# Attention products per head in 32-column tiles, V in chunks of 128 tokens, packs in two loads

## The chip, the cores and the metric

One core of one Trainium2 chip runs the whole program. The metric is the device time of one execution in microseconds (us). On the core, TensorE (PE in the profile; PEld is its loading of the stationary operand), VectorE (DVE), ScalarE (ACT), GpSimd (POOL) and SyncE (SP, which issues most DMAs) each work through a list of instructions in order and wait for each other by semaphores.

## What is computed

Three layers follow each other: attention through packs, a mixture of 4 experts with given weights, and a mixture of 8 experts of which each token takes two. The change is in the first.

```python
def _attn_ref(q, k, v, p):          # q, k, v: (4, 8, 576, 64); p: (4, 8, 32, 64)
    def sm_attn(qq, kk, vv):
        s = scale * np.matmul(qq, kk.transpose(0, 1, 3, 2))
        a = np.exp(s - np.max(s, axis=-1, keepdims=True))
        a = a / (np.sum(a, axis=-1, keepdims=True) + 1e-09)
        return np.matmul(a, vv)
    p_packed = sm_attn(p, k, v)
    return sm_attn(q, p_packed, p_packed)
```

For each of 4 batches and 8 heads, 32 packs attend to 576 tokens, and then the 576 tokens attend to the 32 packs. The result, 2304 tokens by 512, goes through both mixtures, whose products are made in two-part float32 (`mm3`, three fp32r matmuls for each product). The attention's own products are plain float32.

## The kernel before

The attention is cut into eight units (`Attn`, one batch `b` and one group `g` of four heads). a0 to a3 are the units of batches 0 and 1; `at_u` holds the four units of batches 2 and 3. A group is two pairs of heads: `hl` is the pair, `h2` the head in it. Since 128 partitions hold two heads of 64 numbers, one matmul over 128 rows works on a pair, and the 128 output rows hold four heads by 32 packs.

A unit has stages. `load_p` (L209) loads the packs (`pc`, 32 KB) and GpSimd spreads them into a zeroed tile `self.p` (L214, L219), so that a pair's matmul writes zeros to the rows of the other pair and the two pairs add up in one PSUM tile. `s1` (L233) makes the scores of the packs, two halves of 288 tokens with two matmuls each, then maximum (DVE) and exponential (ACT). `ext` (L254) transposes the exponentials on TensorE, in five chunks of CH = 116 tokens (the last has 112), and ACT copies them to `a1t`. `pv` (L266) multiplies by v, five matmuls of 256 columns: each head's row meets all four heads' v, and L272 scales and multiplies by a mask that keeps each head's own 64 columns. `pt` (L275) transposes the result, two transposes, and ACT and GpSimd make the tiles `PTr`, `PTh`, `PTl` of it; `PTr` has a zeroed middle part, so that `s2a` (L289) can take 128 columns of it with zeros on one side and add the two pairs up. `s2a` gives the scores of the tokens; `s2b` to `s2f` are the softmax over 32 packs with 32x32 transposes on DVE and the two-part split into `AT`, which the first mixture reads.

Two places hold all this. In the start, ahead of the first mixture, the code calls the stages of a0 to a3 and the first weights' loads (`w_load`, L123, SP) and splits (`w_split`: ACT makes the high part at L68, GpSimd or VectorE the low part at L69) in an order written by hand (L389 to L451). Then the main loop of the first mixture runs, and a list of places (`at(place, f)`) puts the rest between its steps: s2a to s2f of a2 and a3, and all stages of the four units in `at_u` (L481 to L494), so four times s1, ext, pv and pt and six times s2a stand in the stream of the mixture's matmuls (L63 to L65). Every load goes through SP's one queue in the order of the calls.

Of the kernel before, what the change touches and what calls it, by code (L numbers as in the profile page):

```python
# [22 lines left out]
CH, NC = 116, 5  # L23
# [5 lines left out]
def tile_pack_attn_moe_moe(ctx: ExitStack, tc: tile.TileContext, qT, kT, pT, vv, dp, noise,  # L29
# [13 lines left out]
    def acc_ps(t=0):  # L43
        # the fifth bank is free for other work while four tiles are summed
        if t == 4:
            return ps.tile([128, 512], F32, name="accx", tag="accx", bufs=1)
        return ps.tile([128, 512], F32, name="acc", tag="acc", bufs=4)
# [24 lines left out]
    ident = consts.tile([128, 128], F32, name="ident")  # L72
    mask = [consts.tile([128, 256], F32, name=f"mask{i}") for i in range(2)]
# [10 lines left out]
    def early_consts():  # L84
        make_identity(nc, ident)
        for par in range(2):
            nc.gpsimd.memset(mask[par], 0.0)
            for slot in range(2):
                for h2 in range(2):
                    c = ((slot ^ par) * 2 + h2) * 64  # L90
                    r = slot * 64 + h2 * 32
                    nc.gpsimd.memset(mask[par][r:r + 32, c:c + 64], 1.0)
# [40 lines left out]
    # step i: 0..127 first mixture, 200..239 its last tiles, 300.. second mixture  # L133
# [53 lines left out]
    # =====================================================================  # L187
# [4 lines left out]
    def pt_alloc(bp):  # L192
        for hp in range(4):
            r = atp.tile([128, 3, 64], F32, name="ptr", tag=f"ptr{hp}", bufs=1)
            nc.gpsimd.memset(r[:, 1, :], 0.0)
            PTr[bp, hp] = r
# [3 lines left out]
    class Attn:  # L200
        """One batch, four heads: rows (slot, head of the pair, pack) of the two pairs."""
# [7 lines left out]
        def load_p(self):  # L209
            b, g = self.b, self.g  # L210
            pc = self.t([2, 32], "pc")
            nc.sync.dma_start(pc, pT[b, :, 2 * g:2 * g + 2, :])
            self.p = self.t([2, 128], "pT")
            nc.gpsimd.memset(self.p, 0.0)  # L214
            for hl in range(2):
                for h2 in range(2):
                    c = (hl ^ (b % 2)) * 64 + h2 * 32
                    r = slice(h2 * 64, h2 * 64 + 64)
                    nc.gpsimd.tensor_copy(self.p[r, hl, c:c + 32], pc[r, hl, :])  # L219
# [13 lines left out]
        def s1(self):  # L233
            o = [self.new_ps() for _ in range(2)]
            for i in range(2):
                for hl in range(2):
                    nc.tensor.matmul(o[i][:, :288], self.p[:, hl, :], self.k[:, hl, i * 288:(i + 1) * 288],
                                     start=hl == 0, stop=hl == 1)
# [15 lines left out]
        def ext(self):  # L254
            a = self.t([NC, 128], "a1t", CH)
            self.a1t = a
            o = self.new_ps()
# [8 lines left out]
        def pv(self):  # L266
            o = self.new_ps()
            for c in range(NC):
                r = CH if c < 4 else S - 4 * CH
                nc.tensor.matmul(o[:, :256], self.a1t[:r, c, :], self.v[:r, c, :], start=c == 0, stop=c == NC - 1)  # L270
            self.pm = self.t([256], "pm")
            nc.vector.scalar_tensor_tensor(self.pm, o[:, :256], self.sm[:, 7:8], mask[self.b % 2],  # L272
                                           op0=OP.mult, op1=OP.mult)

        def pt(self):  # L275
            o = self.new_ps()
            bp = self.b // 2
            for hl in range(2):
                nc.tensor.transpose(o[:, hl * 128:(hl + 1) * 128], self.pm[:, hl * 128:(hl + 1) * 128], ident)
            for hl in range(2):  # L280
                s = hl ^ (self.b % 2)
                hp = 2 * self.g + hl
                src = o[:, hl * 128 + s * 64:hl * 128 + s * 64 + 64]
                nc.scalar.activation(PTr[bp, hp][:, 2 * s, :], src, AF.Copy)
# [782 lines left out]
```

## Time and profile before

| | |
|---|---|
| three runs | 1268.83, 1271.12, 1272.71 us; median 1271.12 |
| span of the profiled execution | 1268.5 us (its own time is not listed) |
| TensorE busy | 1220.7 us, 96% |
| DVE, ACT, POOL busy | 38%, 37%, 39% |
| DMA | 121.24 MB, mean 96 GB/s |
| chain that ended last | PE 82%, DMA 8%, DVE 4% |

How to read it: the span is the time from the first to the last instruction of one execution. The busy share is a mean over the whole program, and a matmul's busy time includes its way through the array, so that matmuls in a stream overlap in the record: the distance of their starts, not their duration, is what one costs there. The chain goes back from the last instruction to what released it, step by step.

### The profile page before, as it was taken

The page shows a single profiled execution, that of the slowest core. Times are in us where ns is not written, and L with a number is a line of the kernel's source. Part 1 is how long each engine was busy: PE and PEld are TensorE (multiplying, and loading weights), DVE is VectorE, ACT ScalarE, POOL GpSimd, SP SyncE. Part 2 cuts the span into 40 slices and gives each one's busy share as a digit, 9 for nine tenths or more (in the row PEclk, how much of TensorE's full clock was granted, in tenths as well). Part 3 has the DMA queues.
Part 4 walks back from the last instruction along what each step waited for, and adds up shares of the span by engine and source line. Part 5 has one row for each costly group of instructions (what it writes and reads, how often), then busy time and mean ns, then how long its engine had stood idle before and what let it go on. Part 6 is the DMA issues. An engine that isn't in the chain of part 4 may idle for free.

```text
span 1268.5 us, 17265 instructions
## 1 busy us (share of the span) xinstructions
PE 1220.7 (96%) x6638; PEld 1060.8 (84%) x6638; DVE 482.3 (38%) x1183; ACT 467.6 (37%) x973; POOL 489.5 (39%) x377
## 2 busy tenths in 40 slices
PE   4789999999999999999999998799999999999997
PEld 2578888888888898888888887689998998989986
DVE  1564333433464622454435345452212132222222
ACT  1453543433433543634425333342233333232321
POOL 2323322312332411314613134234575757557554
PEclk7999999999999999999999999899999999999999
DMA  5331321321221311212242204454252544535332
GB/s 151 107 128 34 89 86 37 105 81 41 96 80 34 125 51 34 67 34 67 37 67 67 66 20 115 129 168 149 74 173 81 168 135 137 170 116 177 114 140 76
DMA packets 51624, 121.24 MB, mean 96 GB/s; under 512 B 18683, under 2 KB 18827, under 8 KB 51537
## 3 DMA queue, kind: packets, MB, share of 16 engines
q1 hardware_dynamic: 41536, 99.97, 26.0%
q0 software_dynamic: 10000, 20.11, 4.9%
q8 instruction: 55, 0.90, 0.3%
q14 instruction: 33, 0.26, 0.1%
HBM read 105.64 MB, written 23.31 MB: 102 GB/s over the span
## 4 chain that ended last, share of the span: by engine, by line
PE 82%; DMA 8%; DVE 4%; issue 2%; ACT 2%; POOL 1%; SPq 0%; DVEq 0%; POOLq 0%; ACTq 0%
PE acc L64 12%; PE acc L63 12%; PE acc L65 12%; PE mm L63 11%; PE mm L65 11%; PE mm L64 11%; PE accx L64 2%; PE accx L65 2%; PE accx L63 2%; DMA qk<-in_kT_dram 2%; DMA gt<-yd,mti 2%; DMA meta<-rr,rsi 1%; PE mm L828 1%; DMA raw<-in_w_dram 1%; DMA raw<-in_m_dram 1%
## 5 line engine op out<-in xcount | busy, mean ns | idle before, releaser
L69 POOL TENSOR_TENSOR w1l<-raw,w1h 128x1024 fp32r<-128x1024 f32 x58 | 139.5, 2405 | 336.2 <-ACT w1h L68 317.2
L69 POOL TENSOR_TENSOR w2l<-raw,w2h 128x1024 fp32r<-128x1024 f32 x61 | 146.5, 2401 | 217.5 <-ACT w2h L68 179.3
L63 PE MATMUL acc<-w2h,hh 128*128 128x512 f32 x448 | 182.0, 406 | 0.9 <-DVE ml L368 0.9
L64 PE MATMUL acc<-w2l,hh 128*128 128x512 f32 x448 | 177.9, 397 | 0.5 <-DVE w2l L69 0.5
L65 PE MATMUL acc<-w2h,hl 128*128 128x512 f32 x448 | 176.9, 395 | 0.0
L500 DVE SCALAR_TENSOR_TENSOR gl<-mm,gh 128x320 fp32r<-128x320 f32 (+2 forms) x128 | 62.9, 491 | 264.2 <-ACT gh L499 264.1
L499 ACT ACTIVATE gh<-mm 128x320 fp32r<-128x320 f32 (+2 forms) x128 | 56.0, 437 | 282.8 <-PE mm L65 282.8
L63 PE MATMUL mm<-xth,w1h 128*128 128x320 f32 (+2 forms) x512 | 158.7, 310 | 0.9 <-DVE gl L500 0.9
L64 PE MATMUL mm<-xtl,w1h 128*128 128x320 f32 (+2 forms) x512 | 158.1, 309 | 0.6 <-DVE xtl L69 0.6
L65 PE MATMUL mm<-xth,w1l 128*128 128x320 f32 (+2 forms) x512 | 157.9, 308 | 0.0
L63 PE MATMUL mm<-ath,mh 128*128 128x288 f32 x512 | 152.5, 298 | 1.0 <-ACT mh L366 0.7
L65 PE MATMUL mm<-ath,ml 128*128 128x288 f32 x512 | 151.2, 295 | 2.1 <-DVE ml L368 2.1
L64 PE MATMUL mm<-atl,mh 128*128 128x288 f32 x512 | 151.2, 295 | 0.0
L500 DVE SCALAR_TENSOR_TENSOR hl<-mm,hh 128x224 fp32r<-128x224 f32 (+1 forms) x256 | 102.0, 421 | 93.3 <-ACT hh L499 92.8
L368 DVE TENSOR_TENSOR ml<-mm,mh 64x512 fp32r<-64x512 f32 x120 | 82.6, 689 | 120.1 <-ACT mh L366 119.6
L499 ACT ACTIVATE hh<-mm 128x224 fp32r<-128x224 f32 (+1 forms) x256 | 91.2, 384 | 93.4 <-PE mm L65 71.0
L63 PE MATMUL acc<-w2h,gh 128*128 128x512 f32 x264 | 108.0, 409 | 3.6 <-ACT gh L499 3.6
L65 PE MATMUL acc<-w2h,gl 128*128 128x512 f32 x264 | 105.1, 398 | 2.0 <-DVE gl L500 2.0
L64 PE MATMUL acc<-w2l,gh 128*128 128x512 f32 x264 | 104.8, 397 | 0.0
L63 PEld LDWEIGHTS mm<-ath,mh 128*128 128x128 f32 x512 | 96.1, 188 | 8.1 <-ACT mh L366 1.1
L65 PEld LDWEIGHTS acc<-w2h,hl 128*128 128x128 f32 x448 | 84.2, 188 | 20.4
L64 PEld LDWEIGHTS mm<-atl,mh 128*128 128x128 f32 x512 | 96.2, 188 | 5.4
(237 smaller groups left out, 2173.7 us busy)
## 6 DMA issues: line engine op xcount, KB each, us to landing
raw<-in_m_dram SPq DMA_DIRECT2D x72, 512.0 KB, 3.6
raw<-in_w_dram SPq DMA_DIRECT2D x64, 512.0 KB, 4.0
yd<-y SPq DMA_DIRECT2D x7, 1280.0 KB, 8.1
v<-in_vv_dram SPq DMA_DIRECT2D x8, 580.0 KB
qk<-in_kT_dram SPq DMA_DIRECT2D x8, 576.0 KB, 4.6
qk<-in_qT_dram SPq DMA_DIRECT2D x8, 576.0 KB, 3.6
x2d<-x SPq DMA_DIRECT2D x18, 256.0 KB, 5.1
xg<-x2d,mti POOLq DMA_INDIRECT x40, 4.0
```

Source lines behind the costliest of these rows:

```text
L63: nc.tensor.matmul(o, ah, bh, start=start, stop=False)
L64: nc.tensor.matmul(o, ah, bl, start=False, stop=False)
L65: nc.tensor.matmul(o, al, bh, start=False, stop=stop)
L69: (eng or nc.vector).tensor_sub(l, x, h.bitcast(F32))
L368: nc.vector.tensor_sub(l[r, g, :], o[r, :], h[r, g, :].bitcast(F32))
L499: nc.scalar.activation(hd, src, AF.Relu)
L500: nc.vector.scalar_tensor_tensor(ld, src, 0.0, hd.bitcast(F32), op0=OP.max, op1=OP.subtract)
L828: nc.tensor.transpose(o[:, d * 128:(d + 1) * 128], XG[j][t][:, d * 128:(d + 1) * 128], ident)
```

## The change

Each head's products are made by themselves. A matmul of s1, pv and s2a now takes 32 columns of stationary operand (one head's packs) and writes 32 of the 128 output rows (`heads()` gives the pair, the head and the rows). The packs come from the host with zeros where the other head of the pair stands, for all units in one tile `pall`, in two loads of 256 KB: batches 0 and 1 ahead of all loads, batches 2 and 3 at the end of the start. GpSimd's spreading of the packs and the zeroed middle of `PTr` are gone. v is cut into chunks of 128 tokens (the last has 64, padded with zeros by the host; GpSimd zeroes the rows of `a1t` that go with them). The mask now only puts a head's 64 columns into the left or right half, and `pt` needs one transpose.

```diff
-CH, NC = 116, 5
+CH, NC = 128, 5
-    mask = [consts.tile([128, 256], F32, name=f"mask{i}") for i in range(2)]
+    mask = consts.tile([128, 2, 64], F32, name="mask")
+    pall = consts.tile([128, NB, 4, 2, 32], F32, name="pall")
...
-            r = atp.tile([128, 3, 64], F32, name="ptr", tag=f"ptr{hp}", bufs=1)
-            nc.gpsimd.memset(r[:, 1, :], 0.0)
-            PTr[bp, hp] = r
+            PTr[bp, hp] = atp.tile([128, 2, 64], F32, name="ptr", tag=f"ptr{hp}", bufs=1)
...
-        def load_p(self):
-            b, g = self.b, self.g
-            pc = self.t([2, 32], "pc")
-            nc.sync.dma_start(pc, pT[b, :, 2 * g:2 * g + 2, :])
-            self.p = self.t([2, 128], "pT")
-            nc.gpsimd.memset(self.p, 0.0)
+        def heads(self):
             for hl in range(2):
                 for h2 in range(2):
-                    c = (hl ^ (b % 2)) * 64 + h2 * 32
-                    r = slice(h2 * 64, h2 * 64 + 64)
-                    nc.gpsimd.tensor_copy(self.p[r, hl, c:c + 32], pc[r, hl, :])
+                    q = 2 * (hl ^ (self.b % 2)) + h2
+                    yield hl, h2, slice(q * 32, q * 32 + 32)
...
             for i in range(2):
-                for hl in range(2):
-                    nc.tensor.matmul(o[i][:, :288], self.p[:, hl, :], self.k[:, hl, i * 288:(i + 1) * 288],
-                                     start=hl == 0, stop=hl == 1)
+                for hl, h2, r in self.heads():
+                    nc.tensor.matmul(o[i][r, :288], pall[:, self.b, 2 * self.g + hl, h2, :],
+                                     self.k[:, hl, i * 288:(i + 1) * 288], start=True, stop=True)
...
             a = self.t([NC, 128], "a1t", CH)
             self.a1t = a
+            nc.gpsimd.memset(a[S - 4 * CH:, 4, :], 0.0)
...
             for c in range(NC):
-                r = CH if c < 4 else S - 4 * CH
-                nc.tensor.matmul(o[:, :256], self.a1t[:r, c, :], self.v[:r, c, :], start=c == 0, stop=c == NC - 1)
-            self.pm = self.t([256], "pm")
-            nc.vector.scalar_tensor_tensor(self.pm, o[:, :256], self.sm[:, 7:8], mask[self.b % 2],
-                                           op0=OP.mult, op1=OP.mult)
+                for hl, h2, r in self.heads():
+                    h = (2 * hl + h2) * 64
+                    nc.tensor.matmul(o[r, :64], self.a1t[:, c, r], self.v[:, c, h:h + 64],
+                                     start=c == 0, stop=c == NC - 1)
+            self.pm = self.t([2, 64], "pm")
+            nc.vector.scalar_tensor_tensor(self.pm, o[:, :64].unsqueeze(1).to_broadcast([128, 2, 64]),
+                                           self.sm[:, 7:8], mask, op0=OP.mult, op1=OP.mult)
...
-            for hl in range(2):
-                nc.tensor.transpose(o[:, hl * 128:(hl + 1) * 128], self.pm[:, hl * 128:(hl + 1) * 128], ident)
+            nc.tensor.transpose(o[:, :128], self.pm.rearrange("p a j -> p (a j)"), ident)
...
             for i in range(2):
-                for hl in range(2):
-                    s = hl ^ (b % 2)
-                    r = PTr[bp, 2 * g + hl].rearrange("p a j -> p (a j)")
-                    nc.tensor.matmul(self.o2[i][:, :288], r[:, s * 64:s * 64 + 128],
-                                     self.q[:, hl, i * 288:(i + 1) * 288], start=hl == 0, stop=hl == 1)
+                for hl, h2, r in self.heads():
+                    nc.tensor.matmul(self.o2[i][r, :288], PTr[bp, 2 * g + hl][:, hl ^ (b % 2), h2 * 32:h2 * 32 + 32],
+                                     self.q[:, hl, i * 288:(i + 1) * 288], start=True, stop=True)
...
+        nc.sync.dma_start(pall[:, 0:2], pT[:, 0:2])
         for u in (a0, a1):
-            u.load_p()
             u.load_k()
             u.load_v()
...
         w_load(("w1", 0, 3), w1_src(0, 3))
+        nc.sync.dma_start(pall[:, 2:], pT[:, 2:])
```

SP's queue at the start of the program before; pc is a unit's packs, qk its k or q, v its v, raw a weight:

```order
1 L212 DMA pc<-in_pT_dram 128x64
2 L223 DMA qk<-in_kT_dram 128x1152
3 L227 DMA v<-in_vv_dram 116x1280
4 L212 DMA pc<-in_pT_dram 128x64
5 L223 DMA qk<-in_kT_dram 128x1152
6 L227 DMA v<-in_vv_dram 116x1280
7 L212 DMA pc<-in_pT_dram 128x64 [waits DMAHW0_49,Pool_49]
8 L223 DMA qk<-in_kT_dram 128x1152
9 L231 DMA qk<-in_qT_dram 128x1152
10 L212 DMA pc<-in_pT_dram 128x64 [waits DMAHW3_49,DMAHW1_49,Pool_49]
11 L223 DMA qk<-in_kT_dram 128x1152 [waits DMAHW2_49,PE_49]
12 L123 DMA raw<-in_w_dram 128x1024
```

And with the change:

```order
1 L387 DMA pall<-in_pT_dram 128x512
2 L213 DMA qk<-in_kT_dram 128x1152
3 L217 DMA v<-in_vv_dram 128x1280
4 L213 DMA qk<-in_kT_dram 128x1152
5 L217 DMA v<-in_vv_dram 128x1280
6 L213 DMA qk<-in_kT_dram 128x1152
7 L221 DMA qk<-in_qT_dram 128x1152
8 L213 DMA qk<-in_kT_dram 128x1152 [waits DMAHW1_49,PE_49]
9 L120 DMA raw<-in_w_dram 128x1024 [waits DMAHW0_49]
10 L217 DMA v<-in_vv_dram 128x1280 [waits DMAHW2_49,PE_49]
11 L221 DMA qk<-in_qT_dram 128x1152 [waits DMAHW3_49]
12 L120 DMA raw<-in_w_dram 128x1024
```

The four small loads became one ahead of everything, v has 128 rows in place of 116, and the loads of a2 no longer wait for GpSimd.

TensorE's list in the main loop, around the first s1 there (accx, acc and mm are PSUM tiles, w2h and w2l a weight's two parts); before:

```order
531 L64 MATMUL acc<-w2l,hh 128x512
532 L65 MATMUL acc<-w2h,hl 128x512
533 L237 MATMUL accx<-qk,pT 128x288 x2
534 L237 MATMUL mm<-qk,pT 128x288 x2
535 L63 MATMUL acc<-w2h,hh 128x512
```

And with the change:

```order
531 L64 MATMUL acc<-w2l,hh 128x512
532 L65 MATMUL acc<-w2h,hl 128x512
533 L227 MATMUL accx<-qk,pall 32x288 x4
534 L227 MATMUL mm<-qk,pall 32x288 x4
535 L63 MATMUL acc<-w2h,hh 128x512
```

The place is the same; four products of 128 output rows became eight of 32 rows with the same 288 columns each.

## Rows read from the trace of the kernel before

**Rows 1.** The page's busy times, and TensorE's busy share in 40 slices.

```profile
PE 1220.7 (96%) x6638; PEld 1060.8 (84%) x6638; DVE 482.3 (38%) x1183; ACT 467.6 (37%) x973; POOL 489.5 (39%) x377
...
PE   4789999999999999999999998799999999999997
```

**Rows 2.** Table by stretches: us, busy (instructions) per engine, clock, DMA share, GB/s.

```profile
0.00:63.50 63.50, 39.63 (x143) 26.71 (x143) 21.63 (x60) 18.80 (x56) 19.38 (x55) 0.84 0.47 129
100.00:420.00 320.00, 319.90 (x1677) 274.78 (x1676) 137.40 (x314) 130.65 (x311) 84.55 (x69) 1.00 0.22 69
```

**Rows 3.** The chain of waits in the start: start us, us, what.

```profile
3.93 23.37 DMA qk<-in_kT_dram
...
34.71 12.52 DMA raw<-in_w_dram
...
47.25 1.07 ACT w1h L68
```

**Rows 4.** Table by stretches, in the start.

```profile
2.00:12.00 10.00, 5.15 (x16) 2.34 (x14) 1.70 (x7) 1.11 (x5) 1.13 (x5) 0.97 0.93 226
14.00:18.00 4.00, 0.47 (x1) 0.50 (x2) 0.00 (x0) 0.00 (x0) 1.50 (x7) 0.50 0.25 90
24.00:30.00 6.00, 2.56 (x6) 1.88 (x7) 0.51 (x3) 0.35 (x2) 1.96 (x9) 0.59 0.26 101
...
76.00:80.00 4.00, 3.30 (x19) 2.50 (x17) 2.61 (x3) 2.31 (x4) 0.00 (x0) 1.00 0.99 391
```

**Rows 5.** DMA issues: count, size of each, us to landing.

```profile
raw<-in_w_dram SPq DMA_DIRECT2D x64, 512.0 KB, 4.0
...
v<-in_vv_dram SPq DMA_DIRECT2D x8, 580.0 KB
qk<-in_kT_dram SPq DMA_DIRECT2D x8, 576.0 KB, 4.6
...
pc<-in_pT_dram SPq DMA_DIRECT2D x8, 32.0 KB, 12.9
```

**Rows 6.** Pool in order of time: start, us, what, idle before and releaser.

```profile
16.21 0.96 POOL L219 COPY pT<-pc 64x32 f32<-64x32 f32 x4 [12.31 <-DMA pc<-in_pT_dram]
```

**Rows 7.** TensorE in order of time, in the start.

```profile
27.44 2.26 PE L237 MATMUL mm<-qk,pT 128*128 128x288 f32 x4 [5.15 <-DMA qk<-in_kT_dram]
...
31.41 2.56 PE L270 MATMUL acc<-v,a1t 116*128 116x256 f32 x10
33.81 0.60 PE L259 MATMUL mm<-ident,ta 128*116 128x128 f32 x4
...
41.11 1.13 PE L237 MATMUL mm<-qk,pT 128*128 128x288 f32 x4
...
48.47 1.46 PE L296 MATMUL acc<-qk,ptr 128*128 128x288 f32 x4
```

**Rows 8.** TensorE in order of time, in the main loop.

```profile
160.30 1.13 PE L237 MATMUL accx<-qk,pT 128*128 128x288 f32 x4
161.27 1.13 PE L237 MATMUL mm<-qk,pT 128*128 128x288 f32 x4
...
173.09 0.27 PE L263 MATMUL mm<-ident,ta 128*112 128x128 f32 x1
...
182.24 2.32 PE L270 MATMUL accx<-v,a1t 116*128 116x256 f32 x10
...
193.23 0.38 PE L279 MATMUL mm<-ident,pm 128*128 128x128 f32 x2
...
442.35 0.40 PE L63 MATMUL mm<-w1h,pth 128*128 128x512 f32 x1
442.58 0.40 PE L64 MATMUL mm<-w1l,pth 128*128 128x512 f32 x1
...
443.05 0.96 PE L584 MATMUL mm<-wg_t,xt 128*128 128x16 f32 x8
```

**Rows 9.** The page's costliest groups: a weight load in the stream.

```profile
L64 PEld LDWEIGHTS mm<-atl,mh 128*128 128x128 f32 x512 | 96.2, 188 | 5.4
```

More of the change, by code (lines that the diff above doesn't have):

```diff
@@ L85, in early_consts @@
         make_identity(nc, ident)
[L86 to L92, printed above, removed]
+        nc.gpsimd.memset(mask, 0.0)
+        for q in range(4):
+            nc.gpsimd.memset(mask[q * 32:q * 32 + 32, q % 2, :], 1.0)
     def late_consts():
@@ L282, in pt @@
                 hp = 2 * self.g + hl
-                src = o[:, hl * 128 + s * 64:hl * 128 + s * 64 + 64]
-                nc.scalar.activation(PTr[bp, hp][:, 2 * s, :], src, AF.Copy)
+                src = o[:, s * 64:s * 64 + 64]
+                nc.scalar.activation(PTr[bp, hp][:, s, :], src, AF.Copy)
                 nc.scalar.activation(PTh[bp, hp][:, s, :], src, AF.Copy)
-                nc.gpsimd.tensor_sub(PTl[bp, hp][:, s, :], PTr[bp, hp][:, 2 * s, :],
+                nc.gpsimd.tensor_sub(PTl[bp, hp][:, s, :], PTr[bp, hp][:, s, :],
                                      PTh[bp, hp][:, s, :].bitcast(F32))
@@ L376, in ps0 @@
             return (acc_ps, acc_ps, mm_ps, acc_ps, mm_ps, lambda: acc_ps(4), acc_ps, mm_ps)[alt[0] % 8]()
-        bufs0 = {t: 2 for t in ("pc", "pT", "v", "pm", "sm2")} | {"qk": 4, "sm": 4, "ta": 3}
+        bufs0 = {t: 2 for t in ("v", "pm", "sm2")} | {"qk": 4, "sm": 4, "ta": 3}
         a0, a1, a2, a3 = [Attn(p0, b, g, ps0, bufs0) for b in range(2) for g in range(2)]
@@ L402, in tile_pack_attn_moe_moe @@
         pt_alloc(0)
-        a2.load_p()
         a2.load_k()
@@ L407, in tile_pack_attn_moe_moe @@
         a1.s1()
-        a3.load_p()
         a3.load_k()
@@ L484, in tile_pack_attn_moe_moe @@
     for u in at_u:
-        at(s + 0.93, u.load_p)
         at(s + 0.93, u.load_k)
@@ L1026, in heads @@
         return a.reshape(NB, 4, 2, S, 64).transpose(0, 2, 4, 1, 3).reshape(NB, 128, 4, S)
-    pt = p.reshape(NB, 4, 2, 32, 64).transpose(0, 2, 4, 1, 3).reshape(NB, 128, 4, 32)
+    pt = np.zeros((2, 64, NB, 4, 2, 32), f)
+    for h2 in range(2):
+        pt[h2, :, :, :, h2] = p.reshape(NB, 4, 2, 32, 64)[:, :, h2].transpose(3, 0, 1, 2)
+    pt = pt.reshape(128, NB, 4, 2, 32)
     vp = np.zeros((NB, 2, NC * CH, 256), f)
```

## The prediction

> **What bounds the kernel now.** I read the page first: TensorE is busy 96% of the span, but the first two slices of its row are not full [rows 1]. The table by stretches then splits the program in two [rows 2]: from 100 to 420 us TensorE is never idle (319.9 of 320 us), so there each microsecond of matmul stream added or removed is one on the end; in the first 63.5 us TensorE works 39.6, so something else sets the end there. The chain of waits says what [rows 3]: 23.4 us behind the loads up to the third k, 12.5 us behind a w1 load, then ScalarE, which splits that w1 and until then holds up everything queued behind it. So the change has to be priced twice, once for a start that waits for DMA, once for a loop that is TensorE stream.
>
> The start's loads have a second story. From 14 to 18 and from 24 to 30 us, with TensorE waiting, the DMA share is 0.25 and 0.26 at 90 and 101 GB/s, while all engines together can do 0.99 at 391 GB/s [rows 4]. A quarter of 16 engines is four. What is outstanding then are the two v loads, the only ones with 116 rows [rows 5]; every other has 128. I read it so: a load of 116 rows is spread over four engines, and what is queued behind it waits for those four. On Pool the second pack load, 32 KB in the queue behind the first v, arrives after 12.31 us of waiting [rows 6].
>
> **The start, step by step.** The sum is made against the profiled execution's span, 1268.5 us. No time of its own is listed for that execution; the fastest run is 1268.83, the median 1271.1, so 2.6 is added at the end. Removed from the queue of loads: four pack loads of 32 KB; added: one of 256 KB in front (half of it zeros), and v grows from 580 to 640 KB. If v uses all engines, the queue is served in order. At the 226 GB/s (221 KB per us) of the busy stretch [rows 4], from 2 us on: packs and k of a0 (832 KB) 5.8; v 8.7; k of a1 11.3; v 14.2; k of a2 16.8 (before, its matmuls began at 27.44 [rows 7]); q 19.4; k of a3 22.0; the first w1 24.3. Then the queue's next entry, v of a2, waits for a0's product with v on TensorE: scores of a2 from 16.8, up to 4.2 us (twice the 2.1 of one half at the half clock of that stretch, [rows 4, 7]), and the product 2.6 [rows 7], so it is issued at 23.6 at the latest, before the queue is empty. v 27.2, q of a1 29.8, the second w1 32.1. Before, ScalarE could begin that split at 47.25 [rows 3]. That is 15.1 earlier.
> Is TensorE in time? From a0's product to the end of a3's scores it took 8.4 us (33.81 to 42.24 [rows 7]), so it comes to a2's product with v at 32.0, together with the split. What follows is the same chain of ScalarE, VectorE and TensorE as before and moves as a whole: **-15**. At 391 GB/s the same list would end at 19.4, but TensorE's own order then holds: k of a2 10.5, its scores 2.1, a0's product 2.3, the 8.4, a2's product 2.3, so a1's second scores, before at 48.47 [rows 7], come at 25.6: 23 is the most that the start can give. I take 15, because 226 is the rate of this very stretch. GpSimd's removed zeroing and copies (0.96 us per unit [rows 6]) lie under the loads and count nothing; its added zeroing of the last rows of a1t waits for the product of the unit before, which TensorE has long done in the loop. In the start it stands ahead of the w1 split, which waits for its load anyway.
>
> **The loop, step by step.** Four units run s1, ext, pv and pt there, six run s2a. A score group (s1 or s2a) is now 4 products of 288 columns, each two instructions: 8 instructions, four of them in 0.97 us, so 0.243 each and 1.94 in all [rows 8]. It becomes 8 products in 32-column tiles, 16 instructions of the same 288 columns. No row here shows two instructions in different columns of the array, so the price is bounded. Above: one after the other, 16 x 0.243 = 3.88, +1.94 a group. Below: four at a time, 0.97, -0.97. I take a value between: the two instructions of one product need the same 32 columns and follow each other, so only the second of one can lie beside the first of the next product. That makes 9 steps of 0.243 for 8 products, 2.18: +0.24 a group, ten groups, **+2.4** (ends -9.7 and +19.4).
> pv: 10 instructions of 256 columns, 0.216 each by the columns and 2.16 in all (2.32 with the end of the last, [rows 8]), become 40 of 64 columns, each a quarter, 0.054. One after the other it is again 2.16; by the same pairing 21 steps, 1.13: -1.03, four groups, **-4.1**. Ends: four at a time 0.54, -6.5 in all; if each of the 40 weight loads costs what those of the 16-column matmuls cost (8 in 0.96 us, 0.12 each at most [rows 8]), 4.8 and +10.6 in all. A load of 32 columns should cost less than one of 128, so I stay near the low end. pt loses one of two transposes, 0.11 us (0.38 against the 0.27 of a single one, [rows 8]), four times: **-0.4**.
> Changing the tile size back and forth has no row either. In the stream matmuls of 512 columns start every 0.23 us and are 0.40 long [rows 8], so 0.17 of each lies under the next, and so do the 0.19 us of its weight load [rows 9]. If nothing may overlap across a change, a change exposes between 0 and 0.36; I take the first part, 0.17. There are 18 groups in the loop (four s1, four pv, six s2a, and four ext, whose last transpose is now 64 wide), 36 changes: **+6.1** (ends 0 and 13).
> The Trainium skill, "TensorEngine Tiling (Array Packing)", section Tiling Modes, says of this that changing the tiling mode drains TensorE. It speaks against this change; by it the end 0 falls away, without it the sum would be 6.1 lower. No run here shows it yet.
>
> Sum: -15.1 + 2.4 - 4.1 - 0.4 + 6.1 = -11.1, so a span of 1257.4 and a time of **1260**.
>
> **The rivals.**
> 1. All four column tiles work side by side. The order of the change speaks for it: neighbours always differ in column, and in the score groups neighbours come in fours. Against it: each product's second half must follow its first. Loop -9.7 - 6.5 - 0.4 + 6.1 = -10.5, start -17 (TensorE comes sooner too): 1271.1 - 27.5 = 1243.6.
> The Trainium skill, "TensorE: Matmul & The Clock Gate", section "Part 3: Packing small matmuls", gives 2.38 times for three 32-column tiles; it says that tiles of different columns do run at once. Its figure is for one instruction per product; the trace here shows two.
> 2. **Slower**: the tiles run one after the other. Place: s1 and s2a in the loop, where TensorE has no idle time to hide it [rows 2]. Price: +19.4 - 0.4 + 6.1 = +25.1. The start gains less too: a0's product ends at 22.9, then come the 8.4, twice 1.94 more and a2's product 2.2, so a1's second scores start at 37.4 in place of 48.47 [rows 7] and, 1.94 longer, end 9 earlier: -9. Net +16: 1287; 1281 if the changes of tile size cost nothing. It decides from about 3.0 us a score group in place of 2.18: each microsecond more costs ten in the loop and some 3.5 in the start (6 us lost for 1.7), and 11.1 over 13.5 is 0.8. For it: no instruction of this trace runs beside another but for a pipeline's 0.17.
> 3. The start gains nothing: v stays slow, or the loads do not set the end. Against: share and rate of [rows 4] fit four engines, and 116 = 4 x 29 has no larger divisor up to 16, where 128 has 16. Loop alone +4.0: 1275.
> The Trainium skill, "DMA: Bandwidth & Descriptors", in the part on how many engines (k), gives exactly that rule of divisors; the share of 0.25 agrees with it.
> 4. pv is bound by its 40 weight loads: +10.6 in place of -4.1, 1274.7, no change. For it: a product now has a quarter of the stream for each weight load.
>
> **How the numbers follow.** 0.3% is 3.8 us, about what a measurement of this kernel can tell from no change: faster is under 1267.3, slower over 1274.9. Chances: forecast 0.45, rival 1 0.20, rival 2 0.23, rival 3 0.07, rival 4 0.05. The forecast's own range, 1246 to 1267, has the start between 15 and 23 and the changes of tile size between 0 and 0.36 each. Both rival 1 (1243.6) and the greater part of rival 2 are needed for 8 in 10, so the range is 1240 to 1284. Faster: 0.43 of the forecast, all of rival 1, 0.01 of the others, 0.64. Slower: rival 2 with 0.22 and half of rival 3, 0.25. The rest, 0.11, within.
>
> **What would show it.** The DMA share never rests at 0.25 in the start, and ScalarE's second w1 split begins near 32 us. A score group in the loop takes 2.2 us of stream (0.97 in rival 1, 3.9 in rival 2), a pv group 1.1. The first matmul after a group starts 0.2 to 0.4 later than the stream's step. I am wrong if the loop from its first matmul to its end is over 10 us longer, or if the second w1 split starts after 40.

## The result and the profile after

The change is faster: 1237.68 us (median of 4 runs, 1235.92 to 1240.64) against 1269.97 (4 runs, 1266.87 to 1272.71) of the kernel before on the same chip, a ratio of 0.975 (95% interval 0.9729 to 0.9771). The direction was the forecast one, but the time lies 2.3 us below the range and 22 below the predicted 1260; of the four rivals, rival 1 (1243.6) is nearest: its loop (10.5 us gained) came near, and its start (17) was too small as well. The profiled execution took 1235.92 us with a span of 1234.1, against 1268.5 before: 34.4 less.

To see where the 34.4 come from, the same matmul of the mixture (L63 to L65, 5952 of them in both programs) is looked up in both traces and its two start times compared:

| matmul | before | after | difference |
|---|---|---|---|
| first product of the first mixture (L63) | 52.46 | 27.72 | -24.7 |
| first product with w2 (L63) | 67.13 | 41.75 | -25.4 |
| after the last s2a of the loop (L64) | 425.44 | 390.14 | -35.3 |
| last matmul | 1261.38 | 1226.99 | -34.4 |

So the start, up to the first product with w2, gives 25.4 (forecast 15, with 23 as the most). The loop, from there to the last s2a, gives 9.9 (forecast: a loss of 4.0), and 0.9 is lost again behind it, in the routing between the mixtures, where the change touches nothing.

**The start.** The table by stretches of the kernel after, in the order of [rows 4] (us, busy and instructions of PE, PEld, DVE, ACT and POOL, clock, DMA share, GB/s):

```profile
2.00:12.00 10.00, 6.25 (x53) 2.46 (x55) 2.73 (x11) 2.47 (x6) 0.37 (x3) 1.00 1.00 393
12.00:20.00 8.00, 5.61 (x119) 3.44 (x115) 2.60 (x12) 5.57 (x19) 2.14 (x4) 0.86 0.91 338
20.00:30.00 10.00, 6.21 (x94) 2.99 (x86) 7.66 (x21) 4.68 (x18) 5.92 (x8) 0.94 0.55 188
```

In the first ten microseconds the engines now move 393 GB/s at a share of 1.00; before, it was 226 at 0.93 [rows 4]. The stretches at a share of a quarter are gone. The second w1 split, which ScalarE began at 47.25 before [rows 3], stands in ScalarE's list after at 22.71, and not at the forecast 32.1 (start, us, engine, line, what, idle before and releaser):

```profile
22.71 1.06 ACT L68 ACTIVATE w1h<-raw 128x1024 fp32r<-128x1024 f32 x1 [3.07 <-DMA raw<-in_w_dram]
```

The chain of waits of the kernel after still goes through the loads there, but through shorter ones (start, us, what): 4.27 us behind the first k and 7.51 behind the w1 load, where [rows 3] have 23.37 and 12.52; and what follows is a chain of ACT and DVE as before.

```profile
1.19 4.27 DMA qk<-in_kT_dram
...
15.18 7.51 DMA raw<-in_w_dram
22.71 1.06 ACT w1h L68
```

TensorE's list in the start: a2's scores, at 27.44 before [rows 7], begin at 11.69; a0's product with v at 13.50 in place of 31.41.

```profile
5.59 0.69 PE L227 MATMUL acc<-qk,pall 128*32 128x288 f32 x8 [0.88 <-DMA qk<-in_kT_dram]
...
11.69 0.69 PE L227 MATMUL mm<-qk,pall 128*32 128x288 f32 x8 [0.97 <-DMA qk<-in_kT_dram]
...
13.50 0.77 PE L262 MATMUL acc<-v,a1t 128*32 128x64 f32 x40 [0.64 <-ACT a1t L251]
```

**The loop.** The matmuls of the mixture ahead of and behind the first s1 and the first pv of the loop, before (the groups between them are in [rows 8]):

```profile
160.07 0.39 PE L65 MATMUL acc<-w2h,hl 128*128 128x512 f32 x1
...
162.48 0.39 PE L64 MATMUL acc<-w2l,hh 128*128 128x512 f32 x1
...
182.01 0.39 PE L65 MATMUL acc<-w2h,hl 128*128 128x512 f32 x1
...
184.63 0.40 PE L64 MATMUL acc<-w2l,hh 128*128 128x512 f32 x1
```

TensorE's list at the same places after:

```profile
133.63 0.39 PE L65 MATMUL acc<-w2h,hl 128*128 128x512 f32 x1
133.95 0.69 PE L227 MATMUL accx<-qk,pall 128*32 128x288 f32 x8
134.46 0.67 PE L227 MATMUL mm<-qk,pall 128*32 128x288 f32 x8
135.06 0.50 PE L63 MATMUL acc<-w2h,hh 128*128 128x512 f32 x1
135.40 0.39 PE L64 MATMUL acc<-w2l,hh 128*128 128x512 f32 x1
...
155.56 0.40 PE L65 MATMUL acc<-w2h,hl 128*128 128x512 f32 x1
155.88 0.77 PE L262 MATMUL accx<-v,a1t 128*32 128x64 f32 x40
156.58 0.50 PE L63 MATMUL acc<-w2h,hh 128*128 128x512 f32 x1
156.91 0.40 PE L64 MATMUL acc<-w2l,hh 128*128 128x512 f32 x1
```

Eight instructions of 288 columns begin at 133.95 and the next eight at 134.46: 0.51 for eight, where the four of one half took 0.97 before [rows 8]. What a group costs is the distance from the L65 ahead of it to the L64 behind it, less two steps of 0.23 that these two would take without it: 135.40 - 133.63 - 0.47 = 1.30 us for s1, against 1.94 before. The pv group costs 156.91 - 155.56 - 0.47 = 0.89, against 2.16. The starts of the single instructions, which the view puts together, show how the time went (us; the first eight of s1, and the first eight of pv):

```
s1  133.949 133.957 133.964 133.969   134.217 134.224 134.230 134.237
pv  155.882 155.889 155.895 155.901   155.962 155.969 155.975 155.982
```

Four instructions, one in each group of 32 columns, begin within 20 ns, and the second instructions of the same four products follow together, 0.27 us later. So all four column tiles work side by side, in both halves of a product.

The time gained in the groups is not all kept. The difference between the traces, followed matmul by matmul, falls by 0.64 at each of ten score groups, 1.27 at each of four pv and 0.11 at each of four pt (11.9 in all), but rises again by 0.43 to 0.65 behind four of the score groups (2.1 in all). The list of TensorE's waits, which is empty from 90 to 420 us in the kernel before, names 1.5 us of it from 63 to 420 us after (us in total, times, longest):

```profile
PE mm L63 <- DVE ml L358: 0.8, 2, 0.6
PE mm L63 <- DVE hl L488: 0.5, 1, 0.5
PE mm L65 <- DVE ml L358: 0.2, 1, 0.2
```

And VectorE's list behind the first s1 shows why: TensorE comes back to the mixture 0.64 sooner and needs the second of these two ml pieces, which ends at 137.27, because the two still follow each other at 1.35 us, as before (161.69 and 163.03 there).

```profile
135.24 0.69 DVE L358 TENSOR_TENSOR ml<-mm,mh 64x512 fp32r<-64x512 f32 x1 [1.34 <-ACT mh L356]
136.59 0.68 DVE L358 TENSOR_TENSOR ml<-mm,mh 64x512 fp32r<-64x512 f32 x1 [0.66 <-ACT mh L356]
```

The page's own lines after, to [rows 1]: TensorE has 22.5 us less work in a span 34.4 shorter, and the first two of its 40 slices are fuller; to [rows 5]: v has 640 KB.

```profile
PE 1198.2 (97%) x6998; PEld 1033.4 (84%) x6998; DVE 481.5 (39%) x1183; ACT 466.9 (38%) x973; POOL 480.0 (39%) x332
...
PE   6899999999999999999999999799999999999997
...
v<-in_vv_dram SPq DMA_DIRECT2D x8, 640.0 KB
```

### The profile page after: what moved, and what is told of

Read it like the earlier page. It is cut to its first block, busy times and chain, and to the rows that moved or that the text cites. A ratio compares the mean times of both kernels' runs of the same rounds, so it can differ in the third digit from the quotient of the medians.

```text
span 1234.1 us, 17933 instructions
## 1 busy us (share of the span) xinstructions
PE 1198.2 (97%) x6998; PEld 1033.4 (84%) x6998; DVE 481.5 (39%) x1183; ACT 466.9 (38%) x973; POOL 480.0 (39%) x332
## 4 chain that ended last, share of the span: by engine, by line
PE 82%; DVE 5%; issue 4%; DMA 3%; ACT 3%; POOL 2%; another core or an unknown queue 0%; POOLq 0%; SPq 0%; DVEq 0%; ACTq 0%
PE acc L63 13%; PE acc L64 13%; PE acc L65 13%; PE mm L63 11%; PE mm L65 11%; PE mm L64 11%; PE accx L64 2%; PE accx L63 2%; PE accx L65 2%; PE mm L816 2%; DMA meta<-rr,rsi 1%; DVE ml L358 1%; PE mm L572 1%; ACT mh L356 1%; DMA raw<-in_w_dram 1%
## 5 line engine op out<-in xcount | busy, mean ns | idle before, releaser
L63 PE MATMUL acc<-w2h,hh 128*128 128x512 f32 x448 | 181.0, 404 | 0.9 <-DVE ml L358 0.9
L64 PE MATMUL acc<-w2l,hh 128*128 128x512 f32 x448 | 178.1, 398 | 0.3 <-DVE w2l L69 0.3
L65 PE MATMUL acc<-w2h,hl 128*128 128x512 f32 x448 | 177.0, 395 | 0.0
L63 PE MATMUL mm<-xth,w1h 128*128 128x320 f32 (+2 forms) x512 | 159.1, 311 | 0.7 <-DVE gl L488 0.7
L64 PE MATMUL mm<-xtl,w1h 128*128 128x320 f32 (+2 forms) x512 | 158.4, 309 | 0.6 <-DVE xtl L69 0.3
L65 PE MATMUL mm<-xth,w1l 128*128 128x320 f32 (+2 forms) x512 | 158.2, 309 | 0.0
L63 PE MATMUL mm<-ath,mh 128*128 128x288 f32 x512 | 153.0, 299 | 2.2 <-DVE ml L358 1.0
L65 PE MATMUL mm<-ath,ml 128*128 128x288 f32 x512 | 151.4, 296 | 0.5 <-DVE ml L358 0.5
L64 PE MATMUL mm<-atl,mh 128*128 128x288 f32 x512 | 151.6, 296 | 0.0
L63 PE MATMUL acc<-w2h,gh 128*128 128x512 f32 x264 | 108.0, 409 | 1.6 <-ACT gh L487 1.6
L65 PE MATMUL acc<-w2h,gl 128*128 128x512 f32 x264 | 105.5, 400 | 2.0 <-DVE gl L488 2.0
L63 PEld LDWEIGHTS mm<-ath,mh 128*128 128x128 f32 x512 | 96.4, 188 | 10.8 <-PE mm L65 1.6
L64 PE MATMUL acc<-w2l,gh 128*128 128x512 f32 x264 | 105.0, 398 | 0.0
L63 PEld LDWEIGHTS acc<-w2h,hh 128*128 128x128 f32 x448 | 84.1, 188 | 22.4 <-issue 3.2
L65 PEld LDWEIGHTS acc<-w2h,hl 128*128 128x128 f32 x448 | 84.3, 188 | 20.5
```

The costliest lines, as they stand in the source:

```text
L63: nc.tensor.matmul(o, ah, bh, start=start, stop=False)
L64: nc.tensor.matmul(o, ah, bl, start=False, stop=False)
L65: nc.tensor.matmul(o, al, bh, start=False, stop=stop)
```

## The experiments

In the table, "start" and "loop" are read as above, against the trace of the kernel before: the shift of the first w2 product, and what the shift gains or loses from there to 425 us. The rest of a span's difference lies behind the loop. Times are medians, ratios are against the kernel before on the same chip with their 95% interval. The edits are against the change, or against the kernel before where that is said.

| run | time | ratio | span | start | loop |
|---|---|---|---|---|---|
| the change | 1237.68 | 0.975 (0.9729 to 0.9771) | 1234.1 | -25.4 | -9.9 |
| e1, before with v in 128 | 1247.12 | 0.9833 (0.9816 to 0.9849) | 1245.7 | -21.6 | -0.1 |
| e2, change with v in 116 | 1255.55 | 0.9895 (0.9878 to 0.9911) | 1253.8 | -3.5 | -9.5 |
| e3, e1 and packs in one load | 1247.39 | 0.9834 (0.9818 to 0.9851) | 1244.8 | -22.7 | -0.2 |
| e4, neighbours in one column | 1242.36 | 0.9798 (0.9782 to 0.9815) | 1239.9 | -21.2 | -5.0 |
| e5, last chunk 128 wide | 1237.86 | 0.9756 (0.9743 to 0.9769) | 1236.0 | -24.2 | -10.0 |
| e6, v in 120 | 1243.70 | 0.9796 (0.9781 to 0.9811) | 1243.5 | -20.0 | -9.7 |
| e7, v in 118 | 1281.40 | 1.0107 (1.0091 to 1.0122) | 1278.5 | +12.1 | +0.1 |
| e8, three chunks a head | 1237.63, one run | | 1235.8 | -24.1 | -8.3 |
| e9, two chunks a head | 1233.12, one run | | 1231.3 | -25.0 | -9.7 |
| e10, s1 behind pv | 1234.27 | 0.9722 (0.9697 to 0.9747) | 1234.1 | -22.9 | -9.7 |
| e11, the change again | 1235.45 | 0.9721 (0.97 to 0.9741) | 1235.7 | -22.3 | -10.0 |

### e1 and e2: one half of the change at a time

e1 is the kernel before with only the chunks of v changed, and the products still across heads; e2 is the change with the old chunks.

```diff
-CH, NC = 116, 5
+CH, NC = 128, 5
...
+            nc.gpsimd.memset(a[S - 4 * CH:, 4, :], 0.0)
...
-                r = CH if c < 4 else S - 4 * CH
-                nc.tensor.matmul(o[:, :256], self.a1t[:r, c, :], self.v[:r, c, :], start=c == 0, stop=c == NC - 1)
+                nc.tensor.matmul(o[:, :256], self.a1t[:, c, :], self.v[:, c, :], start=c == 0, stop=c == NC - 1)
```

> The kernel before with v alone in chunks of 128 tokens (a1t's last rows zeroed, five full products); packs, matmuls and order as before. Theory A (the start waits for v loads that use four engines, and these also slow the other loads): the DMA rate from 2 to 12 us rises from 226 to about 390 GB/s, the first w2 matmul of the main loop starts some 20 to 25 us sooner than 67.1, the loop keeps its length within 2 us, time 1246 to 1251. Rival B (the packs ahead of all loads make the start shorter, GpSimd's wait for the small pack loads being the first one of the chain): the start gains under 8 us, time over 1262. Rival C (226 GB/s is what this stretch gives): the start gains about 15, time near 1255.

```diff
-CH, NC = 128, 5
+CH, NC = 116, 5
...
-            nc.gpsimd.memset(a[S - 4 * CH:, 4, :], 0.0)
...
+                n = CH if c < 4 else S - 4 * CH
...
-                    nc.tensor.matmul(o[r, :64], self.a1t[:, c, r], self.v[:, c, h:h + 64],
+                    nc.tensor.matmul(o[r, :64], self.a1t[:n, c, r], self.v[:n, c, h:h + 64],
```

> The changed kernel with v in chunks of 116 tokens again; column tiles and packs in two loads stay. Theory A: the loop is 9 to 11 us shorter than before, the start hardly (0 to 6 us), the DMA share rests at 0.25 in the start, the rate from 2 to 12 us is near 226 GB/s; time 1254 to 1261. Rival B: the start is as short as in the changed kernel, time 1238 to 1243.

The two halves fall apart cleanly: e1 has the start (-21.6) and nothing in the loop, e2 the loop (-9.5) and 3.5 of the start, little more than the starts of one kernel differ by (25.4 for the change, 22.3 for e11). The first ten microseconds by stretches, of e1 and then of e2:

```profile
2.00:12.00 10.00, 8.81 (x29) 4.86 (x27) 2.63 (x11) 1.11 (x5) 4.98 (x27) 1.00 0.98 358
```

```profile
2.00:12.00 10.00, 3.84 (x24) 1.35 (x22) 1.70 (x7) 2.36 (x5) 0.17 (x2) 0.94 1.00 259
12.00:20.00 8.00, 2.95 (x20) 1.47 (x21) 1.12 (x4) 0.00 (x0) 0.00 (x0) 0.50 0.67 179
20.00:30.00 10.00, 3.37 (x59) 1.83 (x57) 1.68 (x8) 1.73 (x6) 0.00 (x0) 0.67 0.23 83
```

With v in 116 rows the engines look busy from 2 to 12 us (0.93 before, 1.00 in e2) and move 226 and 259 GB/s; with 128 rows the same share moves 358 (e1, where 390 was expected) to 393. The traces' records of single packets show the same: a row of k or q is one packet of 4608 bytes, a row of v one of 5120. From 2 to 12 us they take 178 and 196 ns (medians) in the change and in e1, but 260 and 368 ns in the kernel before, 285 and 348 in e2. So the v loads of 116 rows also cost the stretch in which they were not alone, and that stretch is where the forecast had taken its rate from.

### e3: the packs alone

e1 with the packs of batches 0 and 1 in one load ahead of all, GpSimd's spreading kept.

```diff
+    pall = consts.tile([128, 2, 4, 32], F32, name="pall")
...
-            pc = self.t([2, 32], "pc")
-            nc.sync.dma_start(pc, pT[b, :, 2 * g:2 * g + 2, :])
+            if b < 2:
+                pc = pall[:, b, 2 * g:2 * g + 2, :]
...
+        nc.sync.dma_start(pall, pT[0:2].rearrange("b p h j -> p b h j"))
```

> e1 with the packs of the first two batches in one load of 128 KB ahead of all others (GpSimd spreads them as before; the later units load theirs as before). Theory A: like e1 within 3 us, since with a fast queue the small loads arrive in time. Rival B: 5 us or more below e1.

The time is that of e1 (1247.39 and 1247.12), and the start 1.1 us earlier in the trace, less than the same kernel's starts differ (22.3 to 25.4 for the change). The packs' loads are no part of the gain that can be measured.

### e4: neighbours in the same columns

The same products, with the loops exchanged, so that a head's products follow each other (in s2a as in s1).

```diff
-            for i in range(2):
-                for hl, h2, r in self.heads():
+            for hl, h2, r in self.heads():
+                for i in range(2):
...
-            for c in range(NC):
-                for hl, h2, r in self.heads():
-                    h = (2 * hl + h2) * 64
+            for hl, h2, r in self.heads():
+                h = (2 * hl + h2) * 64
+                for c in range(NC):
...
```

> The changed kernel with its products in another order, same products and tiles: a score group makes both halves of 288 tokens of one head before the next head, a product with v all five chunks of one head before the next, so neighbours in the list mostly share their 32 columns. Theory A1 (matmuls start in the order of the list, and only neighbours in different columns run side by side): of 16 score instructions only those at three borders can pair, 13 steps of 0.243 = 3.2 us and the two changes 0.3, against 1.3 in the changed kernel, so ten groups cost 22 us more in the loop, pv 37 steps of 0.054, 2.0 against 0.7, 5 us more; time 1262 to 1270. Rival A2 (each column of the array works through its own list and the order does not matter): within 2 us of 1237.7.

Neither expectation came out whole. The score groups stay four wide (four columns side by side), and cost 0.02 us more each; pv does not. Its rows in the loop:

```profile
160.17 0.39 PE L65 MATMUL acc<-w2h,hl 128*128 128x512 f32 x1
160.49 1.84 PE L262 MATMUL accx<-v,a1t 128*32 128x64 f32 x40
162.26 0.50 PE L63 MATMUL acc<-w2h,hh 128*128 128x512 f32 x1
162.60 0.40 PE L64 MATMUL acc<-w2l,hh 128*128 128x512 f32 x1
```

That is 1.96 us by the same reckoning, against 0.89. The single starts: the first instruction of each column begins at 160.492, 160.857, 161.222 and 161.586, each 0.006 after the seventh of the ten instructions of the column before it (160.851, 161.216, 161.581). My reading: instructions are handed out in the order of the program, and a column holds one that runs and three that wait. The tenth of a column is placed when the seventh starts, and only then does the next column get its first. Since every product is two instructions, one running and one waiting product would look the same in these runs. A score group has four instructions for each column in a row and so never stops. The loop keeps 5.0 of 9.9; four times 1.07 are 4.3 of the missing 4.9.

### e8 and e9: how much a column can hold

The change with pv's chunks taken three at a time for each head (six instructions in a row in one column), and two at a time (four).

```diff
-            for c in range(NC):
+            for c0 in range(0, NC, 3):
...
+                    for c in range(c0, min(c0 + 3, NC)):
```

> The changed kernel with the product with v in another order: three chunks of one head, then three of the next head, and so on, then the remaining two chunks alike, so six and four instructions of one column of the array follow each other in the list. Read from e4: with ten in a row the next column began 0.365 us after the one before, as its seventh instruction had started. Theory A3 (matmuls are handed out in the order of the list; a column holds one running and three waiting, and a fourth stops the handing out for all): six in a row hold up the next column by two steps, four by none; 16 steps of 0.056 in place of 10, so a product with v takes 0.34 us more than the changed kernel's 0.70, 1.0 to 1.1. Rival A2 (the columns are independent over some longer reach): 0.70. Rival A1 (only neighbours in the list pair): 40 instructions less the 7 borders, 33 steps, 1.8 to 2.

```diff
-            for c in range(NC):
+            for c0 in range(0, NC, 2):
...
+                    for c in range(c0, min(c0 + 2, NC)):
```

> As e8 with two chunks of one head at a time, so four instructions of one column in a row (two for the fifth chunk). Theory A3: one running and three waiting is just enough, so the product with v takes the 0.70 us of the changed kernel, within 0.05. Rival A1: 40 instructions less some 11 borders, 29 steps, 1.6 to 1.8.

Rows of e8 and then of e9, pv in the loop and the matmul behind it:

```profile
157.20 1.17 PE L263 MATMUL accx<-v,a1t 128*32 128x64 f32 x40
158.30 0.50 PE L63 MATMUL acc<-w2h,hh 128*128 128x512 f32 x1
```

```profile
156.33 0.80 PE L263 MATMUL accx<-v,a1t 128*32 128x64 f32 x40
157.07 0.50 PE L63 MATMUL acc<-w2h,hh 128*128 128x512 f32 x1
```

From the first of the 40 to the next matmul it takes 1.10 us with six in a row, 0.73 with four, 0.70 in the change with two and 1.77 in e4 with ten. Four fit, six don't, as the reading from e4 had forecast (1.0 to 1.1, and 0.70 within 0.05). e8's loop gains 1.6 less than the change's, four times the 0.40. e9's one run has the shortest span of all, but its loop gains no more than the change's (9.7 and 9.9), and of the 37.2 that it is shorter than the kernel before 2.6 come in the routing: no gain from this order is shown.

### e6 and e7: v on other numbers of engines

The change with chunks of 120 and of 118 rows (the rest as in e2).

```diff
-CH, NC = 128, 5
+CH, NC = 120, 5
```

> As e2 (column tiles and packs stay), with v in chunks of 120 tokens. 120 = 15 x 8, 116 = 4 x 29. Theory A (a load runs on as many engines as the largest divisor of its rows up to 16): 15 engines, the DMA share near 0.9 while only v is outstanding, the start as in the changed kernel within 2 us, time 1236 to 1241. Rival (the loads are fast because all 128 partitions are written): the start of e2, 1255.

```diff
-CH, NC = 128, 5
+CH, NC = 118, 5
```

> As e2 with chunks of 118 tokens. 118 = 2 x 59. Theory A: two engines. While only v is outstanding the DMA share is 0.125 at some 50 GB/s; one v load of 590 KB then takes 12 us by itself where e2 has 6, four of them stand one behind the other in the start, so the start is some 20 to 30 us longer than e2's and the time 1273 to 1290. Rival (any load of fewer than 128 rows is slow alike): 1254 to 1258.

e7 has two rows a chunk more than e2 and is 24.7 us longer by the spans, 1.1% slower than even the kernel before; its time lies within the forecast of theory A. While only v is under way, the share is an eighth, two engines of 16:

```profile
10.00:12.00 2.00, 0.00 (x0) 0.00 (x0) 0.34 (x3) 0.00 (x0) 0.00 (x0) 0.50 0.13 54
```

118 is 2 x 59, 116 is 4 x 29 and 120 is 15 x 8: the number of engines is the largest divisor of the rows up to 16. The packet records show it directly: in the first 60 us the number of v's packets under way at the same time is most often 4 in the kernel before, 2 in e7, 15 in e6 and 16 in the change. The Trainium skill, "DMA: Bandwidth & Descriptors", in the part on how many engines (k), states this rule of divisors; the shares of 0.25 and 0.13 and these packets agree.

In e7 the loop kept nothing of its 9.9 either, which was not expected. TensorE waits 8.6 us in it for VectorE's ml, 7.7 of them in two places. In both the chain leads back over ScalarE to a weight load that SP issued behind a load of v and that took 13.08 us (from 161.19) and 13.49 us (from 254.14), where 4.0 is the median before [rows 5]. Behind both the granted clock is lower (a mean of 0.62 from 178 to 182 us and of 0.57 from 271 to 275). So there, too, v on two engines holds up what is queued behind it.

e6 takes 1243.7 where theory A had 1236 to 1241, and its start is that of neither e2 (the rival is out) nor quite the change. Its first stretch:

```profile
2.00:12.00 10.00, 4.74 (x28) 1.58 (x30) 1.70 (x7) 2.36 (x5) 0.17 (x2) 0.81 1.00 274
```

All engines look busy and move 274 GB/s, 0.7 of the change's 393, though 15 of them carry v. In that stretch a packet of v takes 360 ns and one of k or q 203 (medians; 196 and 178 in the change). In e7, with v on two engines, both have the change's medians, 196 and 178. So packets do not simply get slower the fewer engines v has; the number of engines is not the whole of it.

### e5: the last chunk as wide as the others

The last chunk takes the last 128 tokens, with zeros in v for the 64 that it shares with the one before; no zeroing, and the fifth transpose is 128 wide (the host's part of the edit, which lays out v, is left out here).

```diff
-            nc.gpsimd.memset(a[S - 4 * CH:, 4, :], 0.0)
...
-            r = S - 4 * CH
-            nc.tensor.transpose(o[:r, :128], self.ex[:, 4 * CH:S], ident)
-            nc.scalar.activation(a[:r, 4, :], o[:r, :128], AF.Copy)
+            nc.tensor.transpose(o[:, :128], self.ex[:, S - CH:S], ident)
+            nc.scalar.activation(a[:, 4, :], o[:, :128], AF.Copy)
...
```

> The changed kernel; the last chunk of v and of the exponentials is now the last 128 tokens (the 64 that chunk four has too are zeros in v), so ext's fifth transpose is 128 wide like the others and nothing has to be zeroed by GpSimd. Read from the trace of the changed kernel: a change of tile size costs 0.1 to 0.2 us of TensorE. Theory A (the change of size costs, whatever the product is): eight changes fewer in the loop, so the loop from the first w2 matmul to its 400th us is 1 to 1.6 us shorter. Rival (only the 32-column products cost at their borders): the loop keeps its length within 0.3 us. Time by A 1235 to 1237.5, too near to the changed kernel's 1237.7 for the runs alone; the starts of the same matmuls in both traces decide.

There is no difference, in time or loop, as the rival had it. An ext group takes 0.69 us from the matmul ahead of it to the one behind with a last transpose 112 (before), 64 (the change) or 128 wide (e5): a narrower transpose is no change of tile size that costs. Four of the forecast's 18 groups with such changes fall away.

### e10 and e11: two groups side by side

e10 is e5 with the s1 of the later three units put right behind the pv of the unit before, so that three pairs of changes between tile sizes fall away; e11 is the change once more, on the same chip.

```diff
-    for u in at_u:
-        at(s + 0.93, u.load_k)
+    for i, u in enumerate(at_u):
+        at(s + (0.93 if i == 0 else -3.07), u.load_k)
...
-            at(s + 0.23, getattr(u, stg))
+            at(s + (0.23 if stg != "s1" or i == 0 else -3.77), getattr(u, stg))
...
```

> e5 with s1 of each later unit put right behind the product with v of the unit before (its k is loaded four steps sooner), so that three pairs of changes of tile size go. Theory A: three times the cost of two changes, 0.3 each, 0.9 us less in the loop than e5. Rival (earlier loads or the longer gap in the mixture's matmuls give it back): no shorter than e5.

> The changed kernel on the same chip as e10, to compare with: 1236 to 1240.

The ratios of the two differ by less than their intervals, and e10's loop is no shorter than e5's (9.7 and 10.0), as the rival had it. In the trace, s1 right behind pv costs 1.17 us in place of 1.30 at two of the three places: 0.13 saved, and not the 0.33 of two changes of tile size. TensorE's list there, and VectorE's row beside it:

```profile
158.43 0.77 PE L260 MATMUL accx<-v,a1t 128*32 128x64 f32 x40
159.02 0.67 PE L227 MATMUL mm<-qk,pall 128*32 128x288 f32 x8
159.68 0.69 PE L227 MATMUL accx<-qk,pall 128*32 128x288 f32 x8
```

```profile
159.27 0.35 DVE L263 SCALAR_TENSOR_TENSOR pm<-accx,sm,mask 128x128 f32<-128x128 f32 x1 [1.56 <-PE accx L260]
```

pv's last four instructions begin at 158.96 and s1's first four 0.056 later, the step of pv's own stream: here, where the tile size does not change, nothing is lost between two groups. But s1's second half needs the one PSUM tile accx, which VectorE reads for pm until 159.62, and begins 0.66 after the first in place of 0.51. At the third place a whole wait comes in:

```profile
202.84 0.69 PE L227 MATMUL mm<-qk,pall 128*32 128x288 f32 x8 [0.97 <-DVE ml L356]
```

So what the merging should give (three times 0.33), waits mostly take back, and no version was found that beats the change by a measurable amount.

## Why the prediction was wrong, point by point

**The start: right mechanism, wrong size.** That v at 116 rows runs on four engines and that the queue behind it waits was right (e1, e2, e7). The step that failed is "at the 226 GB/s of the busy stretch": the forecast took it as the rate of this very stretch, but it was a symptom of the same cause. With v on 16 engines it is 393, and the second w1 split came 9.4 us before its forecast time. The forecast's other end, worked out at 391 GB/s, was 23; measured are 25.4, and 22.3 in e11. The choice between the two ends was the mistake: a rate that is measured while the suspected brake is on does not hold once the brake is gone.

**The loop: wrong mechanism.** The step that failed is that the two instructions of a product must follow each other, and only neighbours overlap. The starts show the second instructions four wide as well, since each column works off its own short list. A score group's stream came to four steps of 0.243, 0.97 (the four-wide end of the bounds; forecast 2.18), and pv's to ten steps of 0.056, 0.56 (that end 0.54; forecast 1.13). The Trainium skill, "TensorE: Matmul & The Clock Gate", section "Part 3: Packing small matmuls", which stood behind rival 1, says that tiles of different columns run at once, and the trace agrees: 16 instructions of 0.243 would be 3.88 in a row and take a quarter of it.

**The changes of tile size: right size on average, too many.** A score group costs 1.30, of which 0.97 is four-wide stream, and pv 0.89, of which 0.56 is; the 0.33 left in both are two changes, 0.165 each on average against the forecast 0.17. That this was the tail of a matmul, as the forecast had it, is not shown, so the size is in part luck: the step into a group is only 0.09 longer than the stream's (133.63 to 133.95, less 0.23), and most of the rest falls behind it. The weight loads suggest another cause. In the kernel before, the load for s1's first matmul at 160.30 begins at 160.08, under the matmul ahead; in the kernel after, the loads at the two borders of s1 begin only with their matmuls, at 133.95 and 135.06, and last 0.11 and 0.19. The Trainium skill, "TensorEngine Tiling (Array Packing)", section Tiling Modes, says that a change of mode drains TensorE, and the 0.33 agree in so far that a change isn't free. But there are 14 groups that pay (not the four ext): 28 changes, 4.6 us, not 6.1.

**pt** gave 0.11 four times, as forecast. **Rival 4** (weight loads) is out: a load of 32 columns lasts 0.11 us, and the 40 instructions with their loads start four to each 0.056 us (156.018 and 156.074 for the third and fourth four of that pv).

**What no case had** are the new waits: TensorE was taken as the only bound of the loop, and it was, to 319.9 of 320 us [rows 2]. But the score groups had covered VectorE's ml pieces. Made 0.64 shorter, four of the ten lost most of that to waits for VectorE. So the loop's sum is -6.4 (s1, s2a) - 5.1 (pv) - 0.4 (pt) + 2.1 (waits) = -9.8, and -9.9 is measured. Rival 1's -10.5 had these very streams; it counted 1.5 for four pairs of changes that cost nothing, and no waits: two errors that nearly cancel.

Together: the start gave 25.4 where 15.1 was forecast (10.3 of the error), the loop came out at -9.9 where +4.0 was forecast (13.9), and 0.9 was lost again in the routing.

## What to carry to other kernels

Read the number of rows of a load against 16 before its bytes: 118 rows in place of 128 cost this kernel 44 us. And a rate taken from a stretch in which a suspect is at work belongs to the suspect; price the change at the rate of an undisturbed stretch as well, and let that be the likelier one if the suspect goes. For products of 32 columns, write the code so that no column gets more than four instructions in a row (two float32 products; six cost 0.40 us a group here, ten 1.07), and look at what waited behind the group that becomes shorter.

## What the runs showed that was not expected

- Engines that look busy moved very different amounts from 2 to 12 us: at a share of 0.93 to 1.00, 226 GB/s in the kernel before and 259 in e2 (116 rows), 274 in e6 (120 rows), and 358 to 393 with 128 rows. The single packets took up to twice as long beside v loads of 116 and 120 rows, but not beside those of 118 rows (e7). Why stays open.
- By the starts in e4, e8 and e9, a column of the array holds one running and three waiting instructions, and instructions are handed out in the program's order: pv takes 0.70, 0.73, 1.10 and 1.77 us with two, four, six and ten in a row.
- The granted clock. In the kernel after it is 0.50, the 1.2 GHz level, from 32 to 38 us, with TensorE busy 5.90 of these 6 us; ahead of that TensorE had been busy 0.54 of two microseconds and 1.12 of two, the latter with a pv in 32-column tiles. It is 0.50 from 28 to 36 us in e5 and from 30 to 38 us in e11, too.

```profile
28.00:30.00 2.00, 0.54 (x3) 0.10 (x2) 1.93 (x5) 0.88 (x3) 1.78 (x3) 1.00 0.53 186
30.00:32.00 2.00, 1.12 (x41) 0.71 (x41) 1.93 (x7) 1.07 (x4) 0.35 (x2) 0.84 0.00 0
32.00:38.00 6.00, 5.90 (x16) 4.20 (x16) 5.62 (x11) 4.69 (x12) 4.19 (x6) 0.50 0.00 1
```

  In e1, with full-width products, it stays at 1.00 from 30 to 40 us, but there TensorE had been busier ahead of it (1.14 and 1.60 of the same two microseconds), so it is not shown whether the narrow products or the idle time lowered the clock. In the kernel after, nine matmuls of 512 columns start every 0.43 us from 32 to 38 us in place of 0.23, which is up to 1.8 us; how much of it VectorE would have taken anyway was not tried.
- The routing behind the loop, which no edit touched, moved the span by -2.6 (e9) to +4.8 us (e6) against the kernel before, and the start of the same kernel by 3 (the change and e11). A single profile tells the loop's gain to a tenth of a microsecond, but the span only to a few.
